# Pairing the lone tiles of batches 4 and 6, and another order in batch 0's token transform

## The chip, the cores and the metric

One core of one Trainium2 chip. The metric is the device time of one launch in microseconds; it is given as the median of several runs. PE is the matrix engine, ACT the scalar engine, DVE the vector engine, POOL the GpSimd engine, SP the engine that issues most DMAs. PSUM is the memory into which PE writes, eight banks of 512 fp32 columns.

## The reference, cut to what matters

Cosine attention over 8 batches, 12 heads, 448 tokens, 64 per head, then a Fourier mix over tokens and channels, then a layer norm and a two-layer perceptron with residual:

```python
q_n = q / (norm(q) + 1e-6);  k_n = k / (norm(k) + 1e-6)
attn = softmax(q_n @ k_n.T / tau);  x = attn @ v          # x: 8 x 448 x 768
u = x + real(fft(fft(x, axis=1), axis=2))                 # tokens, then channels
un = (u - mean(u)) / sqrt(var(u) + 1e-6)
out = u + relu(un @ w_ch1) @ w_ch2                        # 768 -> 3072 -> 768
```

## The kernel before, in words

All of it is one program that is unrolled in Python. Every step is an operation of a small planner (`Plan`): an engine or a choice of engines, a duration, a priority, the names it reads and writes. `Plan.schedule` runs a list scheduler over its own model of the engines and the DMA queues and writes out the order of the instructions of each engine by hand; `Plan.emit` then issues them in that order with semaphores between the engines. So each engine works its list strictly in order, and a late instruction holds up all behind it. The dictionary `SHIFT` adds a number to the priority of single operations, by name; `LATE` adds time to what the planner assumes of operations that wait for a DMA; `TIMES` holds the durations. `Plan.fill` puts dummy matmuls into gaps of PE.

For each batch b there are three parts.

*Attention, `attn(b)`.* Norms of q and k, loads by SP into STG (W2b and TX for batches 0 and 1), squares on ACT (L883), sums on DVE (L885), scaling on POOL into QH (L896), transposes by DMA. Then six head pairs, in the order `ORDER`: the scores are a matmul on 64 rows per head (L973), the exponentials are on ACT (L951), the products with v are L1004 and L1010, the division is on DVE, and `fold` (L1047, L1054, L1081) makes the sums and differences that the channel transform uses. The scores of a head pair come in steps: each step takes one large PSUM tile ("G", two banks, three of them) for each of its key tiles. Batches 1 to 3 take steps of two key tiles, which reach over to the next head pair, batches 4 to 7 steps of three.

*Fourier mix, `fft(b)`.* `fsum` (L1129 to L1138) is the token transform on PE, evacuated into Tt by ACT and DVE (L1160, the `te` operations); `fft` multiplies by the channel tables on PE (`fd0` and `fd1`, L1181 to L1191). In batch 0 each of `fd0` and `fd1` is two groups of matmuls, the cosine sums first and the sine sums second; both read the table CSd, whose negated sine part POOL writes (`sinp`, L659) from the plain sine table CSp. DVE adds the result to x and gives U with its row sums (L1233, in batch 0 L1245). Then each tile of 128 rows gets its mean (L1270), its sum of squares on ACT (L1275), logarithm and exponential for the root (L1278, L1280), and DVE centres and scales it into UN (L1282, `un`). In batch 0, tile 0, the scaling comes later and `un` only centres. UN lies in the buffer F and is transposed into UNT, by PE and two copies in batch 0 (L1292, L1300, `tn` and `eu`), by a DMA transpose on SP's queue in the others (L1303, `tru`). UNT has four slots of 128 columns.

*Perceptron, `ffn(b)`.* Tiles are worked in units of two tiles or one. Even batches have three tiles, odd ones four (their last tile, Zt, shares its buffer with the batch before). The up projection of a pair has 144 matmuls with 256 columns (`up`, L1350), that of a lone tile 144 with 128; the ReLU that evacuates them is on ACT or DVE (L1366). Three pairs at the end (the pair of batch 6 and both of batch 7) use `ups` (L1445), a Strassen scheme with 252 matmuls of 128 columns, whose weight sums DVE makes in `wsums` and `wsum3` in the buffers STG, QH and QK. The down projection (`prod`, L1494) takes seven products of 12 matmuls with 384 columns for a pair (Strassen again, with combinations of the hidden tiles on DVE, L1593, by `comb`), and four for a lone tile. Results of a pair are partly copied by ACT (L1514), added to by POOL (L1519) and by DVE (L1530) in `fin`, and stored by `store`: by SP, or by POOL as an indirect DMA (L1552).

`units` sets the slots, and `ffn` the units: a lone tile and a pair in batches 0 and 6, a pair and a lone tile in batches 2 and 4, two pairs in odd batches.

In `build` the program is laid out as attention of batch 0, then for each b the transform of b, the attention of b + 1 and the perceptron of b. The matmuls of the perceptron are one chain (`self.main`) with the lowest priority on PE, so they fill what attention and transform leave.

Of the kernel before, what the change touches and what calls it, by code (L numbers as in the profile page):

```python
# [7 lines left out]
AluOp = mybir.AluOpType  # L8
# [17 lines left out]
TF = 4  # L26
ORDER = (0, 1, 2, 3, 5, 4)
# [51 lines left out]

SHIFT = {  # L80
    "iotad": {0: 76.7149}, "tpd": {1: 15.2941}, "ktd0": {0: 169.0303}, "ix3": {0: -59.6164}, "ix4": {0: 735.3976}, "vz1": {0: 116.8365},
    "pads": {0: 761.6515}, "sins": {0: 15.0098}, "ldt0": {0: 217.8585}, "ldt1": {0: -95.8889}, "sind": {0: -207.551}, "sinp": {0: 240.8715},
# [418 lines left out]
class Kern:  # L501
# [663 lines left out]
    def fft(self, b):  # L1165
# [94 lines left out]
        for ui, ut in enumerate(order):  # L1260
# [24 lines left out]
            if b == 0 and ui == 0:  # L1285
                self.un0 = un
# [271 lines left out]
    def ffn(self, b):  # L1558
# [42 lines left out]
        for i, two in ((0, 0), (1, 1)) if b == self.nb - 2 else [(i, i + 1 < len(tiles)) for i in range(0, len(tiles), 2)]:  # L1601
            if two:
# [7 lines left out]
                for k in range(3):  # L1610
                    comb(4, 2, 3, [k], AluOp.add, "s1")
# [186 lines left out]
```

## Time and profile before

| | |
|---|---|
| runs | 577.16, 578.32, 577.0 us; median 577.16 |
| profiled execution | span 575.2 us from the first to the last instruction; the page gives no other time for it |
| PE busy | 555.8 us, of which 13.26 us are filler matmuls (L1737), nearly all before 48.3 us |
| DVE, ACT, POOL busy | 430.6, 385.3, 220.3 us |
| first up projection of batch 0 | 48.46 us |
| first matmul of batch 0's channel transform | 43.79 us |
| last down projection ends | 571.8 us |

A line of the page names the line of the program, the engine, the operation, what it writes and reads, shapes and count. In the rows of the order of an engine the first number is the start and the second the length. Matmuls are pipelined and their ends are modelled, so a single one's length in those rows is longer than the distance to the next; the rows of the chain that ended last give that distance over a run of them.

### The profile page before, as it was taken

How to read it: one execution, taken by the hardware profiler on the slowest of the kernel's cores; microseconds unless marked ns; L12 is line 12 of the kernel's file. 1: busy time of each engine (PE TensorE's matmuls, PEld its weight loads, DVE VectorE, ACT ScalarE, POOL GpSimd, SP SyncE). 2: the span in 40 equal slices, each digit the busy share in tenths (PEclk: the TensorE clock that was granted, in tenths of full speed). 3: DMA queues.
4: the chain of work that ended last, by engine and by line, in shares of the span. 5: the costliest groups of instructions: out<-in, count | busy, mean ns of one | idle time of the engine just before them, and what ended most of it. 6: DMA issues, size and time to landing. Idle time of an engine off the chain costs nothing.

```text
span 575.2 us, 16313 instructions
## 1 busy us (share of the span) xinstructions
PE 555.8 (97%) x6766; PEld 436.2 (76%) x6766; DVE 430.6 (75%) x917; ACT 385.3 (67%) x724; POOL 220.3 (38%) x332
## 2 busy tenths in 40 slices
PE   3899999999999999999999999999999999989997
PEld 3569787676787686878788787778778787959694
DVE  8989968996669869975669669776778579986262
ACT  7898885564876885687558875577637853747270
POOL 7534414356329544612370724523270210041303
PEclk9999999999999999999999999999999999999999
DMA  9999999975459739952595429743591210023001
GB/s 188 224 233 171 166 186 130 171 152 111 111 94 103 178 76 135 142 127 62 112 121 93 102 80 147 150 84 85 89 113 29 43 57 28 2 43 72 28 28 56
DMA packets 187898, 62.20 MB, mean 108 GB/s; under 512 B 166800, under 2 KB 185616, under 8 KB 187824
## 3 DMA queue, kind: packets, MB, share of 16 engines
q1 hardware_dynamic: 129856, 38.35, 33.7%
q0 software_dynamic: 57968, 22.81, 30.9%
q8 instruction: 53, 0.87, 0.6%
q14 instruction: 21, 0.17, 0.1%
HBM read 51.90 MB, written 11.01 MB: 109 GB/s over the span
## 4 chain that ended last, share of the span: by engine, by line
PE 60%; DVE 4%; ACT 2%; issue 0%; DVEq 0%; ACTq 0%
PE PS L1494 23%; PE PS L1350 20%; PE PS L1445 6%; PE PS L1010 4%; PE PS L973 3%; DVE U L1233 1%; PE PS L1004 1%; PE PS L986 1%; ACT E L951 1%; DVE ACG L1222 1%; ACT F L1275 1%; PE PS L1134 1%; PE PS L1191 1%; DVE SM L885 1%; DVE HQ L1593 1%
## 5 line engine op out<-in xcount | busy, mean ns | idle before, releaser
L1350 PE MATMUL PS<-UNT,W1b 128*128 128x256 bf16 (+1 forms) x1872 | 186.1, 256 | 1.2 <-DMA UNT<-F 0.6
L1350 PEld LDWEIGHTS PS<-UNT,W1b 128*128 128x128 bf16 x1872 | 155.5, 98 | 20.1 <-issue 2.7
L951 ACT ACTIVATE E<-PS 128x900 bf16<-128x900 f32 (+1 forms) x192 | 148.0, 827 | 19.1 <-PE PS L973 16.6
L1494 PE MATMUL PS<-W2b,HQ 128*128 128x384 bf16 x768 | 133.1, 326 | 0.0
L896 POOL TENSOR_TENSOR QH<-STG,SM 128x256 bf16<-128x256 f32 x126 | 82.3, 679 | 91.9 <-DVE SM L702 73.3
L1494 PEld LDWEIGHTS PS<-W2b,HQ 128*128 128x128 bf16 x768 | 73.3, 98 | 46.2 <-issue 0.7
L1519 POOL TENSOR_TENSOR OUTB<-OUTB,U 128x192 f32<-128x192 f32 x66 | 43.2, 675 | 138.5 <-ACT OUTB L1514 137.3
L1366 ACT ACTIVATE HQ<-PS 128x512 bf16<-128x512 f32 x81 | 48.2, 595 | 40.0 <-PE PS L1350 39.5
L1494 PE MATMUL PS<-TX,HQ 128*128 128x384 bf16 (+2 forms) x408 | 69.7, 321 | 1.8 <-ACT MV L1278 1.6
L883 ACT ACTIVATE QH<-STG 128x384 f32<-128x384 f32 x84 | 42.7, 520 | 25.8 <-DVE SM L885 21.3
L1494 PEld LDWEIGHTS PS<-TX,HQ 128*128 128x128 bf16 x408 | 38.4, 98 | 25.7 <-ACT MV L1278 2.0
L1593 DVE TENSOR_TENSOR HQ<-HQ 128x1536 bf16<-128x1536 bf16 (+1 forms) x69 | 49.5, 721 | 9.9 <-ACT HQ L1366 7.1
L885 DVE TENSOR_REDUCE SM<-QH 128x6 f32<-128x384 f32 x84 | 44.7, 544 | 11.3 <-ACT QH L883 11.0
L1010 PE MATMUL PS<-VB,E 128*128 128x65 bf16 x1152 | 51.4, 193 | 0.0
L1366 DVE TENSOR_SCALAR HQ<-PS 128x512 bf16<-128x512 f32 x45 | 31.0, 688 | 23.8 <-PE PS L1350 23.4
L1010 PEld LDWEIGHTS PS<-VB,E 128*128 128x128 bf16 x1152 | 47.7, 97 | 1.2
L1552 POOL DMA_INDIRECT out_dram<-OUTB,IDX x21 | 23.8, 1134 | 56.9 <-DVE OUTB L1530 51.7
L1004 PE MATMUL PS<-VZ,E 128*128 128x130 bf16 x192 | 41.6, 219 | 0.5 <-ACT E L951 0.2
L973 PE MATMUL PS<-QK 64*128 64x225 bf16 (+2 forms) x864 | 39.6, 227 | 0.1
L1233 DVE SCALAR_TENSOR_TENSOR U<-ACG,X 128x768 bf16<-128x768 f32 (+4 forms) x39 | 39.1, 1015 | 0.8
L1530 DVE TENSOR_TENSOR OUTB<-PS,OUTB 128x384 f32<-128x384 f32 x33 | 18.2, 553 | 25.7 <-PE PS L1494 21.9
L1514 ACT ACTIVATE OUTB<-PS 128x384 f32<-128x384 f32 x33 | 16.1, 488 | 29.5 <-PE PS L1494 29.1
(191 smaller groups left out, 793.6 us busy)
## 6 DMA issues: line engine op xcount, KB each, us to landing
STG<-in_q_dram SPq DMA_DIRECT2D x18, 384.0 KB, 4.0
STG<-in_k_dram SPq DMA_DIRECT2D x18, 384.0 KB, 3.8
VB<-in_v_dram POOLq DMA_DIRECT2D x24, 192.0 KB, 7.1
W1b<-in_moe_w_ch_dram POOLq DMA_DIRECT2D x12, 384.0 KB, 7.7
W2b<-in_moe_w_ch_dram POOLq DMA_DIRECT2D x12, 384.0 KB, 7.2
out_dram<-OUTB SPq DMA_DIRECT2D x7, 384.0 KB, 3.4
W2b<-in_q_dram SPq DMA_DIRECT2D x2, 576.0 KB, 10.0
W2b<-in_k_dram SPq DMA_DIRECT2D x2, 576.0 KB, 10.7
```

What stands on the lines that cost most here:

```text
L885: P.add("dve", lambda v, o=SS[:, i, H // ns * x:H // ns * (x + 1)], sq=sq: v.tensor_reduce(o, sq.rearrange("p (h d) -> p h d", d=DH), AX.X ...
L896: r = v.tensor_tensor(v3(qh)[:, h:h + 4], v3(buf)[:, h:h + 4], RN[:, i, h:h + 4].unsqueeze(2).to_broadcast((128, 4, DH)), AluOp.mult)
L951: return a.activation(o, self.PS[:, bk:bk + nc_, 0:SQ2], ACTF.Exp, scale=1.0 / self.tau)
L973: i = pe.matmul(self.PS[:, bk + h, c0:c0 + n], self.KT[r, jj, kt * 128:(kt + 1) * 128], self.QT[r, jj, cols], start=True, stop=True)
L1004: r = pe.matmul(o, st(6), self.VZ[:, j, :], start=not split, stop=(split and i == 0), skip_group_check=True)
L1010: r = pe.matmul(o[:, 65 * h:65 * h + 65], st(2 * kt + h), self.VB[:, kt, 2 * j + h, :], start=(split and i == h == kt == 0), stop=((not sp ...
L1233: self.snu.append(P.add("dve", lambda v: v.scalar_tensor_tensor(two(U[o0:o0 + n, ut, :]), src, 1.0, two(X[i0:i0 + n, x, :]), AluOp.mult, A ...
L1350: r = pe.matmul(self.PS[:, bk, x * n:(x + 1) * n], self.W1b[:, j, ft * 128:(ft + 1) * 128], self.UNT[:, j, cs], start=(j == 0), stop=(j == ...
L1366: return e.activation(o, i, ACTF.Relu) if e is self.nc.scalar else e.tensor_relu(o, i)
L1494: r = pe.matmul(self.PS[:, bk, 0:n], lhs(f), rhs(f), start=(start and f == 0), stop=(stop and f == NF // 2 - 1), skip_group_check=True)
L1519: r = g.tensor_tensor(self.OUTB[:, ob, xs], self.OUTB[:, ob, xs], self.U[:, ut, xs], AluOp.add)
L1593: P.add("dve", lambda v: v.tensor_tensor(cs(o), cs(a), cs(bq), op), 0.16 + 0.3 * len(ks), -0.5, f"{nm}{ks[0]}_{b}", reads=rd, writes=[x fo ...
```

## The change

1. *Units.* `units` now goes through all tiles in order and makes pairs, except for the tiles in `ONES`, batch 0's first and batch 2's first, which stay alone. A pair may reach from a batch into the next. Batch 2 has its lone tile ahead of its pair. Batch 4's third tile is paired with batch 5's first, batch 5's second with its third, batch 5's fourth with batch 6's first. A unit belongs to the batch of its last tile. `fin` and `store` take the batch of the tile.
2. *The held tile.* Batch 5's fourth tile (`HELD`) isn't centred in `fft(5)`; `unheld` does it after the up projection of the pair ahead, into one of the six QH buffers in place of UN, with its transpose on SP's queue.
3. *Batch 0's transform.* The sine sums, which read CSp, come first in `fd0` and `fd1`; the negated table gets a name of its own, CSm, for which only the other groups wait.
4. *Halves.* Batch 0's first tile is centred in two halves of 384 columns, transposed in two groups of three matmuls, and each copy waits for its own group.
5. *Scores of batch 3* come in steps of three key tiles.
6. *Order.* `LATE` assumes later DMAs for four kinds of operations; the first scores of a batch are ordered behind the last channel transform matmuls of the batch before; `QUEUES` pins the order of the first loads on SP's and POOL's queues; `SHIFT` has entries for nearly all operations of all batches, so that the lists of all engines are drawn anew. One write of the tail's output (`finz`) names one buffer more.

```diff
+ONES = ((0, 0), (2, 0))
+HELD = (5, 3)
...
+QUEUES = [("ld_q1_0 ld_k0_0 ld_q0_0 ld_t0_0 ld_q2_0 ld_t1_0 ld_k1_0 ld_t2_0 ld_k2_0 ld_q0_1 ld_t0_1 ld_k0_1 ld_k1_1 ld_t1_1 ld_q1_1"),
+          ("ld_v2_0 ld_v0_0 ld_v1_0 ld_v3_0 W1_0 W1_1 W1_2 W1_3 W1_4 W1_5 W1_6 W1_7 W1_8 W1_9 W1_10")]
...
-LATE = {r"W[12]_\d+": 1.5, "tmd": 2.0, r"sq\d_\d": 1.5, ... r"ktd\d": 2.0, r"qdup\d": 2.0, ...
+LATE = {r"sq6_[2-7]": 4.0, r"W[12]_\d+": 1.5, "tmd": 2.0, r"sq\d_\d": 2.0, ... r"ktd\d": 3.5, r"qdup\d": 4.0, ...
...
-            ... "sinp", reads=["CSp"], writes=["CSd"])
+            ... "sinp", reads=["CSp"], writes=["CSm"])
...
-            elif b >= 4:
+            elif b >= 3:
                 steps = [[(pos, kt) for kt in range(3)]]
...
-                      ... order=([self.last_qk] if self.last_qk else []) + self.pvs[-2:-1])
+                      ... order=([self.last_qk] if self.last_qk else []) + self.pvs[-2:-1] + (self.fd_ops[-1:] if b and pos == 0 else []))
...
-            for sg in (0, 1) if b == 0 else (0,):
+            for sg in (1, 0) if b == 0 else (0,):
                 self.fd_ops.append(P.add("pe", ..., f"fd{kt}_{b}",
-                                         reads=["Tt0", "Tt1", "Tt1b", "CSd"] + (["CSp"] if b == 0 and sg else []),
-                                         tiles=(tile,), acquire=None if sg else tile, margin=0.2))
+                                         reads=["Tt0", "Tt1", "Tt1b", "CSd"] + ([["CSm"], ["CSp"]][sg] if b == 0 else []),
+                                         tiles=(tile,), acquire=tile if sg or b else None, margin=0.2))
...
-            fds = self.fd_ops[-2:]
+            fds = self.fd_ops[-2:][::-1]
...
+            if (b, ui) == HELD:
+                self.held = (ut, rn, lp, slot, col)
+                continue
+            halves = [slice(0, 384), slice(384, DM)] if late else [slice(0, DM)]
+            for g, c in enumerate(halves):
+                un = P.add("dve", lambda v, ...: v.tensor_scalar(self.UN[:, nb_, c], U[:, ut, c], self.MV[:, ut, 0:1], ...), ... f"un{ui}_{b}", ...)
             if b == 0:
                 tile = Tile("G")
+                tns = []
+                for g in range(2) if late else (None,):
+                    def fn(pe, tile=tile, nb_=nb_, g=g):
+                        for j in range(NJ) if g is None else range(3 * g, 3 * g + 3):
+                            r = pe.matmul(...)
+                    tns.append(P.add("pe", fn, 0.2 if late else 0.4, lp, f"tn{ui}_{b}", ...))
                 for g in range(2):
...
-                    self.evac(ev, 384, lp, f"eu{ui}{g}_{b}", writes=[f"uT{slot}" + "xy"[g]], after=(tile.users[0],), tiles=(tile,))
+                    self.evac(ev, 384, lp, f"eu{ui}{g}_{b}", writes=[f"uT{slot}" + "xy"[g]], after=(tns[g if late else 0],), tiles=(tile,))
...
+    def unheld(self):
+        P = self.P
+        ut, rn, lp, slot, col = self.held
+        b, ui = HELD
+        r = self.qh_next % 6
+        self.qh_next += 1
+        qn = [f"QH{r}"] + ["QH1x"] * (r == 1) + ["QH4x"] * (r in (3, 4))
+        P.add("dve", lambda v: v.tensor_scalar(self.QH[:, r, :], self.U[:, ut, 0:DM], self.MV[:, ut, 0:1], self.RS[:, ut:ut + 1], AluOp.add, AluOp.mult),
+              t_dve(DM, 4) + 0.16, lp, f"un{ui}_{b}", reads=rn + [f"MV{ut}", f"RS{ut}"], writes=qn)
+        self.last_tru = P.add("sp", lambda sy, sem: sy.dma_start_transpose(self.UNT[:, :, col:col + 128], self.QH[:, r, :]).then_inc(sem, 16), ...)
...
-        self.slots, u = [], 0
-        for b in range(self.nb):
-            sl = []
-            for n in (1, 2) if b in (0, self.nb - 2) else (2, 2) if b % 2 else (2, 1):
-                sl += [2 * (u % 2) + x for x in range(n)]
-                u += 1
-            self.slots.append(sl)
+        self.slots = [[0] * len(self.tiles(b)) for b in range(self.nb)]
+        order = [(b, i) for b in range(self.nb) for i in range(len(self.tiles(b)))]
+        u = x = 0
+        self.pairs = []
+        while x < len(order):
+            n = 1 if order[x] in ONES else 2
+            for y in range(n):
+                b, i = order[x + y]
+                self.slots[b][i] = 2 * (u % 2) + y
+            self.pairs.append(order[x:x + n])
+            u, x = u + 1, x + n
...
-        for i, two in ((0, 0), (1, 1)) if b == self.nb - 2 else [(i, i + 1 < len(tiles)) for i in range(0, len(tiles), 2)]:
+        for k, unit in enumerate([u for u in self.pairs if u[-1][0] == b]):
+            two = len(unit) == 2
...
-                if b >= self.nb - 2:
+                if b == self.nb - 1 or unit[0] == (self.nb - 2, 1):
                     if not last_b:
                         self.wsum3()
...
-                    self.up(b, (i, i + 1), chunks, True)
+                    self.up(b, unit, chunks, True)
+                    if unit[1][0] == HELD[0] and unit[0][0] < b:
+                        self.unheld()
...
+        named = {op.name: op for op in self.P.ops if op.dma is not None}
+        for q in QUEUES:
+            q = [named[n] for n in q.split()]
+            for x, y in zip(q, q[1:]):
+                y.order += (x,)
```

More of the change, by code (lines that the diff above doesn't have):

```diff
@@ L977, in attn @@
                 self.last_qk = P.add("pe", fn, 0.195 * len(st_) + 0.2, pj, f"qk{j}{st_[0][1]}_{b}", reads=rd,
-                      tiles=new, acquire=new, margin=0.3, order=([self.last_qk] if self.last_qk else []) + self.pvs[-2:-1])
+                      tiles=new, acquire=new, margin=0.3, order=([self.last_qk] if self.last_qk else []) + self.pvs[-2:-1] + (self.fd_ops[-1:] if b and pos == 0 else []))
                 for tile, (ps, kt) in zip(new, st_):
@@ L1055, in fold @@
                        t_dve(512, 2) + (0.03 if b else 0.0), pj, f"f{eo}{dj}_{b}", reads=["AC0", "AC2"],
-                       writes=[f"F{eo}{dj}"] + ([f"UN{x}" for x in range(4)] if dj == 0 and eo == 0 else []),
+                       writes=[f"F{eo}{dj}"] + ([f"UN{x}{y}" for x in range(4) for y in ("", "h")] if dj == 0 and eo == 0 else []),
                        after=[self.first_f] if dj or eo else [])
@@ L1285, in fft @@
-            if b == 0 and ui == 0:
-                self.un0 = un
+            if (b, ui) == HELD:
[3 more added lines that the diff above has]
+            for g, c in enumerate(halves):
+                un = P.add("dve", lambda v, ut=ut, nb_=nb_, late=late, c=c: v.tensor_scalar(self.UN[:, nb_, c], U[:, ut, c], self.MV[:, ut, 0:1], None if late else self.RS[:, ut:ut + 1],
+                                                                                          AluOp.add, AluOp.bypass if late else AluOp.mult),
+                      t_dve(c.stop - c.start, 4) + 0.16, lp, f"un{ui}_{b}", reads=rn + [f"MV{ut}"] + [f"RS{ut}"] * (not late), writes=[f"UN{nb_}" + "h" * g] + [f"UN{nb_}h"] * (not late))
@@ L1287, in fft @@
             if b == 0:
                 tile = Tile("G")
-                def fn(pe, tile=tile, nb_=nb_):
-                    for j in range(NJ):
-                        r = pe.matmul(self.PS[:, self.bank(tile) + j // 3, 128 * (j % 3):128 * (j % 3) + 128],
-                                      self.UN[:, nb_, 128 * j:128 * j + 128], self.ID, start=True, stop=True)
-                    return r
-                P.add("pe", fn, 0.4, lp, f"tn{ui}_{b}", reads=[f"UN{nb_}", "ID"], tiles=(tile,), acquire=tile)
+                tns = []
@@ new lines, in fft @@
+                for g in range(2) if late else (None,):
+                    def fn(pe, tile=tile, nb_=nb_, g=g):
+                        for j in range(NJ) if g is None else range(3 * g, 3 * g + 3):
+                            r = pe.matmul(self.PS[:, self.bank(tile) + j // 3, 128 * (j % 3):128 * (j % 3) + 128],
+                                          self.UN[:, nb_, 128 * j:128 * j + 128], self.ID, start=True, stop=True)
+                        return r
+                    tns.append(P.add("pe", fn, 0.2 if late else 0.4, lp, f"tn{ui}_{b}", reads=[f"UN{nb_}" + "h" * (g == 1), "ID"] + [f"UN{nb_}h"] * (g is None), tiles=(tile,), acquire=None if g else tile))
@@ L1337, in up @@
         P = self.P
-        sl = [self.slots[b][i] for i in idx]
+        sl = [self.slots[x][i] for x, i in idx]
         n = 128 * len(sl)
@@ L1531, in fin @@
         on = f"OUT{ob}" + "b" * c + "z" * (c0 > 0)
-        return self.P.add("dve", fn, t_dve(c1 - c0), -1, f"{nm}_{b}", reads=([on] if src == "out" else self.unames(b, ut)) + [f"RS{ut}"] * late, writes=[on],
+        return self.P.add("dve", fn, t_dve(c1 - c0), -1, f"{nm}_{b}", reads=([on] if src == "out" else self.unames(bt, ut)) + [f"RS{ut}"] * late, writes=[on],
                           after=(op,), tiles=(tile,))
@@ L1562, in ffn @@
         if b == 0:
-            self.up(0, (0,), range(0, NF, 4), False)
-            self.up(0, (1, 2), range(0, NF, 2), True)
+            self.up(0, ((0, 0),), range(0, NF, 4), False)
+            self.up(0, ((0, 1), (0, 2)), range(0, NF, 2), True)
             for i, ut in enumerate(tiles):
@@ L1614, in ffn @@
                 op = self.prod(b, b1, H(0), W(0, 0), hr(0), wr(0), f"m1{i}", True, False)
-                rd = self.fin(b, b1, op, 0, 0, u0, "a", f"fa{i}")
+                rd = self.fin(b, b1, op, 0, 0, u0, "a", f"fa{i}", bt=b0)
                 comb(0, 4, 0, range(3), AluOp.subtract, "s2")
                 op = self.prod(b, ta, H(1), W(1, 0), hr(1), wr(1), f"m2{i}", True, True)
-                self.fin(b, ta, op, 0, 0, u0, "out", f"fin{i}0")
-                if last_b and i + 2 == len(tiles):
-                    self.store(b, i, u0, 0, 0)
+                self.fin(b, ta, op, 0, 0, u0, "out", f"fin{i}0", bt=b0)
+                if lone:
+                    self.store(b0, i, u0, 0, 0)
                 comb(1, 1, 0, range(3), AluOp.subtract, "s4")
                 op = self.prod(b, b1, H(0), TT(1), hr(0), tr(2), f"m6{i}", False, False, rd)
-                rd = self.fin(b, b1, op, 0, 1, u0, "a", f"fv{i}")
+                rd = self.fin(b, b1, op, 0, 1, u0, "a", f"fv{i}", bt=b0)
                 op = self.prod(b, tb, H(4), TT(0), hr(4), tr(1), f"m5{i}", True, False)
@@ L1628, in ffn @@
                 rd = self.fin(b, b1, op, 1, 1, u1, "out", f"fin{i + 1}1")
-                if last_b and i + 2 == len(tiles):
+                if lone:
                     self.store(b, i + 1, u1, 1, 1)
                 op = self.prod(b, tb, H(1), W(1, 1), hr(1), wr(1), f"m3{i}", False, True, rd2)
-                self.fin(b, tb, op, 0, 1, u0, "out", f"fin{i}1")
-                self.store(b, i, u0, 0, 1 if last_b and i + 2 == len(tiles) else None)
-                if last_b and i + 2 == len(tiles):
+                self.fin(b, tb, op, 0, 1, u0, "out", f"fin{i}1", bt=b0)
+                self.store(b0, i, u0, 0, 1 if lone else None)
+                if lone:
                     tz, cz = Tile("G"), slice(256, 384)
                     pre = P.add("dve", lambda v: v.tensor_tensor(self.OUTB[:, 1, cz], self.PS[:, self.bank(b1), cz], self.U[:, u1, cz], AluOp.add), t_dve(128), -1,
-                                f"finz_{b}", reads=self.unames(b, u1), writes=["OUT1z"], after=(m7,), tiles=(b1,))
+                                f"finz_{b}", reads=self.unames(b, u1), writes=["OUT1z", "OUT1"], after=(m7,), tiles=(b1,))
                     op = self.prod(b, b1, H(3), lambda f: self.TX[:, 2, f, 0:256], hr(3), tr(4), f"m4{i}", False, True, rd, n=256, more=[pre])
@@ L1649, in ffn @@
                 continue
-            u0 = tiles[i]
-            self.up(b, (i,), (0, 12, 4, 16, 8, 20), False)
+            self.up(b, unit, (0, 12, 4, 16, 8, 20), False)
             comb(4, 0, 2, range(3), AluOp.add, "s5")
```

40 lines of the change are left out of this document (22 added, 18 removed), and 503 rows, old and new, of tables (SHIFT, TIMES).

## The prediction

> **What bounds the kernel now.** I read the profile's page first: the busy shares and the clock in 40 slices.
>
> ```profile
> span 575.2 us, 16313 instructions
> PE 555.8 (97%) x6766; PEld 436.2 (76%) x6766; DVE 430.6 (75%) x917; ACT 385.3 (67%) x724; POOL 220.3 (38%) x332
> PEclk9999999999999999999999999999999999999999
> ```
>
> PE is busy for 97% of the span, and the granted clock stays at full speed, so idle time or work on PE is what can be taken away. That busy time counts filler matmuls too, so next I asked for the windows by stage, PE's own waits from 48 us on, and the order of PE, ACT, DVE and POOL around the first up projection.
>
> ```profile
> 48.40:117.90 69.50, 68.15 (x790) 52.67 (x789) 57.80 (x136) 51.87 (x107) 26.04 (x37) 1.00 1.12 161
> 117.90:194.90 77.00, 76.73 (x787) 58.01 (x788) 60.40 (x118) 52.47 (x100) 40.66 (x51) 1.00 0.73 120
> 333.20:368.40 35.20, 35.20 (x374) 27.56 (x372) 25.57 (x55) 19.47 (x35) 17.24 (x25) 1.00 0.84 101
> 368.40:388.30 19.90, 19.82 (x302) 15.76 (x300) 15.58 (x39) 15.21 (x35) 4.15 (x7) 1.00 0.53 127
> 484.60:516.10 31.50, 29.86 (x371) 24.15 (x369) 28.29 (x64) 20.62 (x48) 5.53 (x7) 1.00 0.16 27
> 571.80:575.20 3.40, 0.00 (x0) 0.00 (x0) 0.29 (x1) 0.00 (x0) 0.27 (x1) 0.88 0.32 116
> ...
> PE PS L1494 <- ACT MV L1278: 1.6, 1, 1.6
> PE PS L1350 <- DMA UNT<-F: 0.6, 1, 0.6
> ```
>
> In a window row the first pair is length and PE busy, then PE loads, DVE, ACT, POOL. Idle PE time between 48.4 and 571.8 adds up to 1.35 + 0.27 + 0.08 + 1.64 and some tenths, 3.5 us in all, and the two longest waits are 2.2 us of it. So the time is: the 48.4 us until the first up projection, some 520 us of matmuls with hardly a hole, and a 3.4 us tail. A matmul that goes away saves its length, as long as the chains on DVE and ACT keep feeding PE.
>
> **The change, part by part.** The sum is made against the span of 575.2 us; the median of the three runs, 577.16, is 1.96 above it, and I carry these 1.96 over. Prices of matmuls come from the chain that ended last, where they stand back to back:
>
> ```profile
> 236.98 4.03 PE PS L1350 x72
> 301.38 9.17 PE PS L1350 x84
> 530.30 13.65 PE PS L1494 x84
> 203.68 0.49 PE PS L973 x8
> 322.65 0.71 PE PS L973 x24
> 204.17 1.42 PE PS L1350 x12
> 213.01 1.31 PE PS L1350 x12
> ```
>
> *Down projection.* A lone tile takes 4 products of 12 matmuls, a pair 7. Batch 4's third tile now goes with batch 5's first, batch 5's fourth with batch 6's first, and the pair (batch 5's tiles 1 and 2) stays a pair: two lone tiles and two pairs become three pairs. 2 x 48 + 2 x 84 = 264 matmuls become 252. At 13.65/84 = 162.5 ns that is -1.95 us.
>
> *Up projection.* The two lone tiles took 288 matmuls with 128 columns, 4.03/72 = 56.0 ns each, 16.1 us; the pair that replaces them takes 144 with 256, 9.17/84 = 109.2 ns each, 15.7 us: -0.4 us. The Strassen form of the up projection stays with the same three pairs.
>
> *Scores of batch 3.* Nine groups of 8 matmuls become six of 12, as batches 4 to 7 have them. 9 x 0.49 - 6 x 0.71 = 0.15 us, and three fewer returns to the up projection, which takes 1.42 instead of 1.31 us for 12 matmuls just behind a group, 3 x 0.11: -0.5 us together. Such a group takes all three large PSUM tiles at once, which batches 4 to 7 do with PE full.
>
> *Start of batch 0's transform.* Both table halves used to wait for the negated table of POOL (L659); now the half that needs only the plain table goes first.
>
> ```profile
> 41.17 2.17 POOL L659 TENSOR_SCALAR CS<-TX 128x770 bf16<-128x770 bf16 x1 [0.31 <-ACT TX L647]
> 42.03 1.33 ACT L1159 ACTIVATE E<-PS 128x900 bf16<-128x900 f32 x2
> 43.79 0.84 PE L1181 MATMUL PS<-CS,E 128*128 128x193 bf16 x8
> 46.56 0.42 DVE L1282 TENSOR_SCALAR F<-U,MV 128x768 bf16<-128x768 bf16 x1
> 48.46 7.79 PE L1350 MATMUL PS<-UNT,W1b 128*128 128x128 bf16 x126
> ```
>
> POOL ends at 43.34, but ACT's evacuation, which the transform needs anyway, ends at 43.36: the first matmul can come from 43.79 to about 43.4, no further. Centring in halves lets three transposes and the first copy begin after the first half. A half takes between 0.21 and 0.42 us, half the row and all of it, so this gains from 0.2 us to nothing. The up projection starts up to 0.6 us earlier. How much of it arrives? The wait of 0.6 us for the transposes of batch 1's tiles (UNT<-F, near 117 us) says that batch 1's chain is already the later one there, with DVE busy 57.8 of 69.5 us. Bounds 0 and -0.6; I take -0.3, the middle, since the rows stand as near to the one as to the other.
>
> *Holes.* The planner's priorities, and so nearly every engine's order, are drawn anew. The 3.5 us of holes can go or stay; nothing in this trace shows which. The largest, 1.64 us, sits where batch 6's last pair meets batch 7's transform and DVE has 28.3 us of work in 31.5. Batch 6 then has a whole pair ahead of that pair in place of a lone tile, so its weight sums can be made earlier. I take half of this hole, -0.8; bounds 0 and -3.5.
>
> *What lies beside.* Per pair in place of two lone tiles DVE gets 4 more combinations, POOL 6 halves of additions, ACT 3 copies:
>
> ```profile
> L1593 DVE TENSOR_TENSOR HQ<-HQ 128x1536 bf16<-128x1536 bf16 (+1 forms) x69 | 49.5, 721 | 9.9 <-ACT HQ L1366 7.1
> L1519 POOL TENSOR_TENSOR OUTB<-OUTB,U 128x192 f32<-128x192 f32 x66 | 43.2, 675 | 138.5 <-ACT OUTB L1514 137.3
> ```
>
> That is 2.9 us on DVE and 4.1 on POOL, costed at nothing, like the three copies, because by the window rows DVE idles between 333 and 388 us for 14 of 55 us, ACT for 20 and POOL for 34. Without that cover DVE's 2.9 us would be the price. Batch 5's held tile is centred into another buffer and transposed later, so on SP's queue its transpose moves past loads of a later batch, and behind it wait loads only; the tile is needed a whole pair (about 40 us) later, the transpose's landing is 2.8 us, so again nothing. Lone before pair in batch 2 asks for one tile instead of two when that batch starts; PE has only 0.27 us of hole up to there, so it gains at most that. The pinned queue orders and the extra ordering behind the last transform repeat an order that the trace already shows on SP, so nothing.
>
> Sum: -1.95 - 0.4 - 0.5 - 0.3 - 0.8 = -3.95, span 571.25, time 573.2.
>
> **The rivals.** *Batch 5 comes late (slower).* Until now the lone tile of batch 4 covered PE while batch 5's transform was finished:
>
> ```profile
> 365.26 1.06 DVE L1233 SCALAR_TENSOR_TENSOR U<-ACG,X 128x768 bf16<-128x768 f32 x1
> DMA to landing us min/median/max: 2.7/2.8/5.3
> 368.42 4.44 PE L1350 MATMUL PS<-UNT,W1b 128*128 128x128 bf16 x72
> 388.30 2.79 PE L1350 MATMUL PS<-UNT,W1b 128*128 128x256 bf16 x24
> 371.38 0.94 ACT L1275 ACTIVATE F<-U,MV 128x768 bf16<-128x768 bf16 x1 [0.24 <-DVE MV L1270]
> 380.32 0.28 ACT L1278 ACTIVATE MV<-MV 128x1 f32<-128x1 f32 x1
> 380.64 0.20 ACT L1280 ACTIVATE MV<-MV 128x1 f32<-128x1 f32 x1
> 380.88 0.48 DVE L1282 TENSOR_SCALAR F<-U,MV 128x768 bf16<-128x768 bf16 x1 [0.22 <-ACT MV L1280]
> ```
>
> After the change the pair with batch 5's first tile is due when batch 4's pair ends, at 368.4 less the 0.8 us saved ahead of it, 367.6. With the transform where it is, the shortest way for that tile is addition, squares, logarithm, root, centring and transpose, 365.26 + 1.06 + 0.94 + 0.28 + 0.20 + 0.48 + 2.8 = 371.0, so 3.4 us of idle PE, less what batch 6's scores fill. Against it: PE ends batch 5's scores at 342.3 but begins its first sums only at 356.95, so there is room to pull the transform forward.
>
> ```profile
> 341.61 0.71 PE PS L973 x24
> 356.95 0.41 PE PS L1134 x8
> ```
>
> What would make it worse is POOL: the same DVE addition took 1.35 us at 366.25 while POOL multiplied, 0.96 at 435.99 while POOL stood idle.
>
> ```profile
> 366.25 1.35 DVE L1233 SCALAR_TENSOR_TENSOR U<-ACG,X 128x768 bf16<-128x768 f32 x1
> 364.33 2.47 POOL L896 TENSOR_TENSOR QH<-STG,SM 128x256 bf16<-128x256 f32 x3
> 435.99 0.96 DVE L1233 SCALAR_TENSOR_TENSOR U<-ACG,X 128x768 bf16<-128x768 f32 x1
> ```
>
> With six more POOL pieces, at 0.4 us each, up to 2.4 us of DVE time would be lost there, and the wait is 5.8 us. Against the safe terms of 3.15 us that gives 577.16 - 3.15 + 5.8 = 579.8; without the slowdown 577.4, no change. It is slower from 4.9 us of wait on. The Trainium skill, page "GPSIMD Engine Reference", section "1. Specifications", has GpSimd's memory interfaces shared with VectorE, contended with two-input DVE instructions; these rows fit it, and it speaks against adding POOL work.
>
> *The saving is lost elsewhere (same).* PE's work falls by 2.85 us, but chains on DVE and ACT do not get shorter; new waits of 1.5 to 2.5 us at the batch boundaries give 576.5. For it: DVE and ACT already hold 6% of the chain that ended last.
>
> ```profile
> PE 60%; DVE 4%; ACT 2%; issue 0%; DVEq 0%; ACTq 0%
> ```
>
> Against it: where PE runs through the pairs of batch 4 the window row has no hole at all.
>
> *All holes go.* 577.16 - 2.85 - 0.6 - 3.5 = 570.2. For it: every order is new; against it: the same DVE load.
>
> *Narrow matmuls wait for their weights.* A load takes 98 ns by itself:
>
> ```profile
> L1350 PEld LDWEIGHTS PS<-UNT,W1b 128*128 128x128 bf16 x1872 | 155.5, 98 | 20.1 <-issue 2.7
> ```
>
> Were the lone tiles' matmuls paced by it, they would cost 288 x 98 ns = 28.2 us, the up term would be -12.5 and the time 577.16 - 1.95 - 12.5 - 0.5 - 1.1 = 561.1. Against it: 72 of them took 4.03 us, so the loads run beside the matmuls. The Trainium skill, page "TensorE: Matmul & The Clock Gate", section "Back-to-back issue gap", takes a middle way, about 81 ns for 128 columns in a stream of loads and matmuls: by it the up term would be -7.6 and the time about 566. This trace disagrees with it, with 56.0 ns.
>
> **How the numbers follow.** Forecast 573.2 (between 571.5 and 575.2): 0.64. All holes go: 0.14. Lost elsewhere: 0.12. Batch 5 late: 0.09. Narrow matmuls paced by loads: 0.01. About 0.3%, 1.7 us, is what a measurement of this kernel tells from no change. Faster is the forecast, the third and the last rival, 0.79; same 0.12; slower 0.09. The range takes in the case without holes down to 570.2, and most of the same-case, to 576.8; that leaves out the late batch, the narrow matmuls and parts of the edges.
>
> **What would show it.** The trace after has 12 matmuls fewer on the line of the down projection and 144 fewer on that of the up projection, and batch 3's scores come in six groups; the first up projection starts before 48.2; between 360 and 375 us PE has no hole of over 1 us; its holes from 48 us to the tail are under 3 us. I would be wrong if PE waited for a transpose of batch 5's first tile, for ACT or DVE at a batch's start, or if the first up projection came no earlier.

## The result and the profile after

The changed kernel took 574.71 us in the median (574.34, 575.18, 573.9, 575.07), the kernel before, beside it, 577.74: ratio 0.9934, 95% interval 0.9922 to 0.9947. It is 3.0 us faster; 573.2 was forecast, a gain of 3.95. The profiled execution took 574.34 us with a span of 572.5. The head of its page:

```profile
span 572.5 us, 15993 instructions
PE 552.2 (96%) x6598; PEld 432.6 (76%) x6598; DVE 439.6 (77%) x926; ACT 382.8 (67%) x723; POOL 231.5 (40%) x338
```

The sum is checked with one window, from the first matmul of the first up projection to the end of PE's last. The kernel before, then the one after (first pair: length, PE busy):

```profile
48.46:571.70 523.24, 519.81 (x6249) 408.39 (x6248) 387.03 (x814) 343.77 (x658) 192.60 (x275) 1.00 0.60 99
```

```profile
48.46:570.06 521.60, 517.29 (x6092) 405.57 (x6092) 396.15 (x824) 341.42 (x658) 204.60 (x281) 1.00 0.68 99
```

Length less busy is the sum of PE's holes, span less the window's end is the tail:

| us | before | after | difference | forecast |
|---|---|---|---|---|
| until the first up projection | 48.46 | 48.46 | 0.0 | -0.3 |
| PE busy | 519.81 | 517.29 | -2.5 | -2.85 |
| holes of PE | 3.43 | 4.31 | +0.9 | -0.8 |
| behind PE's last matmul | 3.47 | 2.47 | -1.0 | 0 |
| span | 575.2 | 572.5 | -2.7 | -3.95 |

Of the 2.7 us by which the profiled span is shorter, 1.6 lie between the first up projection and PE's last matmul (523.24 to 521.60), where the sum had 3.65, and 1.0 lie behind it.

The work of PE is there nearly as counted. The next rows are groups by line and shape of the kernel after: the up projection has 1440 + 288 matmuls where there were 1296 + 576, the down projection 1212 in 720 + 420 + 48 + 12 + 12 (two small last forms, not shown) where there were 1224.

```profile
L1758 PE MATMUL PS<-UNT,W1b 128*128 128x256 bf16 x1440 | 167.9, 273 | 0.7 <-ACT KTD L1230 0.4 <-DVE MV L1657 0.3
L1902 PE MATMUL PS<-W2b,HQ 128*128 128x384 bf16 x720 | 124.8, 326 | 0.0
L1902 PE MATMUL PS<-TX,HQ 128*128 128x384 bf16 x420 | 74.6, 326 | 1.6 <-DVE OUTB L1939 1.4 <-DVE HQ L2002 0.3
L1758 PE MATMUL PS<-UNT,W1b 128*128 128x128 bf16 x288 | 17.4, 219 | 0.5 <-DMA UNT<-F 0.3 <-ACT UNT L1691 0.2
L1902 PE MATMUL PS<-W2b,TX 128*128 128x384 bf16 x48 | 8.1, 326 | 0.0
```

PE's own waits inside that window, after the change (total, times, longest):

```profile
PE PS L1902 <- DVE OUTB L1939: 1.4, 2, 1.0
PE PS L1521 <- DVE F L1485: 0.7, 1, 0.7
PE PS L1758 <- ACT KTD L1230: 0.4, 1, 0.4
PE PS L1758 <- DVE MV L1657: 0.3, 1, 0.3
PE PS L1758 <- DMA UNT<-F: 0.3, 1, 0.3
```

The 1.64 us ahead of batch 7 is gone altogether. In its place stand smaller waits at places that had none. Two of them show what feeds them. Timeline rows of the kernel after around the longest, DVE, POOL and PE (start, length; idle time before and its releaser in brackets):

```profile
189.82 0.56 DVE L1939 TENSOR_TENSOR OUTB<-PS,OUTB 128x384 f32<-128x384 f32 x1 [1.70 <-POOL OUTB L1928]
...
182.83 3.75 POOL L1283 TENSOR_TENSOR QH<-STG,SM 128x256 bf16<-128x256 f32 x4
186.72 2.99 POOL L1928 TENSOR_TENSOR OUTB<-OUTB,U 128x192 f32<-128x192 f32 x4
...
190.44 1.31 PE L1902 MATMUL PS<-TX,HQ 128*128 128x384 bf16 x7 [1.01 <-DVE OUTB L1939]
```

PE waits for DVE's output addition, that one for POOL's, and POOL's stood behind four scalings of the next batch. These additions are of batch 1, whose two pairs are the same before and after; only their place in POOL's order is new. The second is PE's 0.7 us for L1485. The eight executions of that line that read F, by duration (min, median, max):

```profile
L1485 DVE TENSOR_TENSOR F<-F x8: 348/354/770, 291.6 to 485.2; 128x388 bf16<-128x388 bf16 x8
```

The slowest ended just ahead of that wait, at 356 us, while POOL multiplied from 352.9 to 357.4; in the kernel before the same eight took 355 to 368 ns. That agrees with the Trainium skill, page "GPSIMD Engine Reference", section "1. Specifications", by which GpSimd's memory interfaces are shared with VectorE, and VectorE instructions with two inputs are among those that contend for them; no run here moved the POOL work away to prove it.

### The profile page after: what moved, and what is told of

It is laid out like the page before. It is cut to its first block, busy times and chain, and to the rows that moved or that the text cites. A ratio compares the mean times of both kernels' runs of the same rounds, so it can differ in the third digit from the quotient of the medians.

```text
span 572.5 us, 15993 instructions
## 1 busy us (share of the span) xinstructions
PE 552.2 (96%) x6598; PEld 432.6 (76%) x6598; DVE 439.6 (77%) x926; ACT 382.8 (67%) x723; POOL 231.5 (40%) x338
## 4 chain that ended last, share of the span: by engine, by line
PE 75%; DVE 17%; ACT 5%; issue 2%; POOL 1%; DMA 0%; DVEq 0%; POOLq 0%; ACTq 0%
PE PS L1902 26%; PE PS L1758 26%; PE PS L1853 6%; PE PS L1397 6%; PE PS L1360 5%; DVE U L1620 3%; DVE HQ L2002 2%; PE PS L1391 2%; ACT E L1338 2%; PE PS L1373 1%; DVE ACG L1609 1%; PE PS L1525 1%; DVE U L1632 1%; DVE OUTB L1939 1%; DVE SM L1272 1%
## 5 line engine op out<-in xcount | busy, mean ns | idle before, releaser
L1902 PE MATMUL PS<-W2b,HQ 128*128 128x384 bf16 x720 | 124.8, 326 | 0.0
L1283 POOL TENSOR_TENSOR QH<-STG,SM 128x256 bf16<-128x256 f32 x126 | 87.4, 720 | 90.9 <-DVE SM L1089 64.7
L1928 POOL TENSOR_TENSOR OUTB<-OUTB,U 128x192 f32<-128x192 f32 x72 | 50.8, 725 | 127.0 <-ACT OUTB L1923 125.8
L1902 PEld LDWEIGHTS PS<-W2b,HQ 128*128 128x128 bf16 x720 | 68.8, 98 | 43.3 <-issue 0.6
L1902 PE MATMUL PS<-TX,HQ 128*128 128x384 bf16 (+2 forms) x444 | 76.7, 322 | 1.6 <-DVE OUTB L1939 1.4
L1902 PEld LDWEIGHTS PS<-TX,HQ 128*128 128x128 bf16 x444 | 41.4, 98 | 28.2 <-DVE OUTB L1939 2.5
L2002 DVE TENSOR_TENSOR HQ<-HQ 128x1536 bf16<-128x1536 bf16 (+1 forms) x73 | 55.1, 758 | 9.1 <-ACT HQ L1774 6.3
L1662 ACT ACTIVATE F<-U,MV 128x768 bf16<-128x768 bf16 x28 | 26.2, 934 | 21.2 <-DVE MV L1657 17.8
L1923 ACT ACTIVATE OUTB<-PS 128x384 f32<-128x384 f32 x36 | 17.6, 488 | 29.5 <-PE PS L1902 29.2
```

Source lines behind the costliest of these rows:

```text
L1283: r = v.tensor_tensor(v3(qh)[:, h:h + 4], v3(buf)[:, h:h + 4], RN[:, i, h:h + 4].unsqueeze(2).to_broadcast((128, 4, DH)), AluOp.mult)
L1902: r = pe.matmul(self.PS[:, bk, 0:n], lhs(f), rhs(f), start=(start and f == 0), stop=(stop and f == NF // 2 - 1), skip_group_check=True)
L1928: r = g.tensor_tensor(self.OUTB[:, ob, xs], self.OUTB[:, ob, xs], self.U[:, ut, xs], AluOp.add)
L2002: P.add("dve", lambda v: v.tensor_tensor(cs(o), cs(a), cs(bq), op), 0.16 + 0.3 * len(ks), -0.5, f"{nm}{ks[0]}_{b}", reads=rd, writes=[x fo ...
```

## The experiments

**The same kernel again, and work taken out or put in with all orders kept.** The planner writes the orders from its own durations, so an edit at the emission of the matmuls leaves every order as it was.

> The changed kernel once more, unaltered, for a second profile. If the shorter stretch behind PE's last matmul (2.43 us against 3.49 in the kernel before) is part of the change, it is 2.4 again, the holes of PE sum to 4.3 us again, the first up projection starts at 48.5 us again, and the ratio is 0.993. If any of the three is a matter of the single execution, it moves by some tenths here, and the tail is somewhere between 2.4 and 3.5 us.

Measured: 575.4 against 578.82 us, ratio 0.9945 (0.9931 to 0.9958). Span 572.5, tail 2.49, holes 4.5 us, of which 1.00 and 0.66 at the same two places; the first up projection at 48.01 instead of 48.46. So tail and holes belong to the program, and the start moves by itself.

```diff
                 for f in range(4 * c, 4 * c + 4):
+                    if nm[0] == "y" and b in (4, 6) and f == 4 * c + 1:
+                        continue
```

> The kernel before with 24 matmuls of 384 columns left out of the down projections of the two lone tiles of batches 4 and 6 (one of each group of four; those tiles' output is incomplete), all orders as they were. Theory 'PE's work passes through': 24 x 162.5 ns = 3.9 us less, ratio 0.9932. Rival 'the chains on DVE and ACT set these stages': new waits of PE take back at least half, 0 to 2 us less, ratio 0.9965 to 1.

Measured: 577.5 us, ratio 0.9986 (0.9969 to 1.0003): 0.8 us, not 3.9 (1.3 by the medians, 577.5 and 578.82). From the first up projection to PE's last matmul its profile is 0.7 us shorter, and PE's holes there are 5.5 us instead of 3.4. The timeline of PE in this run shows where the rest went:

```profile
369.93 4.45 PE L1350 MATMUL PS<-UNT,W1b 128*128 128x128 bf16 x72
...
383.21 0.78 PE L973 MATMUL PS<-QK 64*128 64x128 bf16 x24 [0.38 <-ACT E L951]
385.51 0.22 PE L1004 MATMUL PS<-VZ,E 128*128 128x130 bf16 x1 [0.44 <-issue]
388.92 2.79 PE L1350 MATMUL PS<-UNT,W1b 128*128 128x256 bf16 x24
...
483.51 2.17 PE L1445 MATMUL PS<-UNT,W1b 128*128 128x128 bf16 x36
486.35 1.26 PE L1445 MATMUL PS<-KTD,QH 128*128 128x128 bf16 x18 [0.66 <-ACT E L1454]
506.83 4.06 PE L1496 MATMUL PS<-TX,HQ 128*128 128x384 bf16 x24 [1.64 <-ACT MV L1278]
516.58 3.62 PE L1445 MATMUL PS<-UNT,W1b 128*128 128x128 bf16 x62
```

Batch 4's lone tile takes 18.99 us instead of 19.88 (368.42 to 388.30 before): 0.9 of 1.95 arrive; most of the rest are a wait for ACT's exponentials and one at 385 us that the profile doesn't name. Batch 6's lone tile is done in the full 1.95 us less, but from there to batch 7's first pair it is 33.07 us instead of 31.47 (484.60 to 516.07): 1.6 of the 1.95 are given back. The one new wait that the profile names there is 0.66 us for ACT's evacuation of the Strassen sums (E, L1454); the 1.64 us for ACT's MV is as long as before. So in the old order a matmul saved at a lone tile was worth little: 'PE's work passes through' fails there.

> The changed kernel with 24 matmuls of 384 columns added (12 ahead of the fifth product of each of the two joined pairs, overwritten by that product), all orders as they were. Theory 'PE's work passes through': 3.9 us more than the changed kernel, ratio to the kernel before 1.000. Rival 'PE waits for DVE and ACT in these stages': the extra work fills holes there (0.3 + 0.0 us stand on the profile between 411 and 484 us, 0.3 in the stretch ahead), and under 2 us arrive, ratio 0.9965 or less.

```diff
+                if (nm, b) in (("m50", 5), ("m50", 6)) and c == 0:
+                    for f in range(12):
+                        pe.matmul(self.PS[:, bk, 0:n], lhs(f % 4), rhs(f % 4), start=True, stop=False, ...)
```

Measured: 579.47 us, ratio 1.001 (1.000 to 1.002), 4.1 us above the unaltered copy in the same comparison. All 3.9 us arrive: no hole in the joined pairs takes up added work. That is one half of the comparison only. Matmuls left out of the joined pairs, and matmuls added to the lone tiles of the kernel before, were not run, so it isn't shown that a saved matmul is worth more in the new order than in the old.

**One part at a time, orders drawn anew.** A run for each of: joining alone with the old priorities; all edits with the old priorities, margins and free queues; the change without the joining (`ONES` with (4, 2) and (6, 0) added, `HELD` off); the change with batch 2's lone tile behind (`ONES = ((0, 0), (2, 2))`). The first still names the table's negated half CSm and keeps one ordering edge of the change, that of a batch's first scores.

> The kernel before with the two lone tiles joined to the tiles of the next batch and nothing else: its own priorities, batch 2's lone tile behind its pair, nine groups of scores in batch 3, the old start. PE has 2.35 us less to do (1.95 down, 0.4 up). Theory 'the work passes through by itself': holes of PE stay at 3 to 4 us, span 572.8, ratio 0.996. Rival 'it needs the orders redrawn': the old priorities on the joined units leave new waits of PE of 2.4 us or more in the stretch from batch 4's last pair to batch 7, ratio 1.000 or more. The stretch behind PE's last matmul stays 3.5 us if the ordering of the last store pieces is what shortened it.

> The changed kernel with all its edits but the priorities, lateness margins and unpinned queues of the kernel before. PE's work is that of the changed kernel, 2.7 us less than before. Theory 'the work passes through by itself': holes 3.5 to 5 us, ratio 0.993 to 0.996. Rival 'it needs the orders redrawn': holes of 7 us or more, ratio 1.000 or more. The tail is 2.5 us if it is the ordering of the last store pieces, 3.5 if it is the drawn order.

> The changed kernel with the joining alone undone: batches 4 and 6 have their lone tiles again, all else (priorities by name, batch 2, scores, start) as changed. PE's work rises by 2.35 us. Theory 'the work passes through': ratio to the kernel before 0.9945 + 2.35/577 = 0.9986. Theory with the chain behind the lone tile of batch 6 (24 matmuls left out gained 1.3 of 3.9 us because PE then waited there for ScalarE and VectorE): the 1.6 us wait ahead of batch 6's last products comes back too, ratio 1.001 to 1.003. Rival 'the gain lies in the new orders and not in the joining': ratio 0.995 as the changed kernel.

> The changed kernel with batch 2's lone tile behind its pair again. The work of PE is the same to 0.1 us. Where the changed kernel waits 1.01 us (189.4 us, for an output addition of batch 1) and 0.30 (193.3, for the transposed tile of batch 2), the holes change: if putting the lone tile first is what opened the 1.01 us hole, it goes and the ratio is 0.993; if it saved a wait for two tiles, a hole of 0.5 to 2 us opens at batch 2's start and the ratio is 0.996 to 0.998; if both are the orders' own, holes differ by under 1 us with no pattern there.

| | median us | ratio, interval | fillers after the first up projection |
|---|---|---|---|
| joining alone | 612.49 | 1.0590 (1.0565 to 1.0616) | 420 |
| old orders | 668.36 | 1.1551 (1.1532 to 1.1569) | 1314 |
| joining undone | 584.63 | 1.0105 (1.0089 to 1.0122) | 90 |
| lone behind | 656.45 | 1.1335 (1.1316 to 1.1353) | 1218 |

All four are slower than the kernel before, by 6 to 90 us. The rival 'it needs the orders redrawn' was on the right side, but none of the expectations came near the size. The busy time of PE misleads here. The window from first up projection to last matmul of the joining alone, and its group of fillers:

```profile
49.44:607.10 557.66, 545.57 (x6507) 429.53 (x6506) 391.82 (x821) 343.89 (x658) 201.76 (x281) 1.00 0.57 93
```

```profile
L1773 PE MATMUL PS<-W1b 128*128 128x128 bf16 x420 | 27.2, 220 | 1.3 <-DVE ACG L1226 0.8 <-DVE U L1237 0.3
```

PE looks busy for 26 us more than before with less to do: the program puts filler matmuls where the planner foresees a hole, 420 here, 6 in both kernels of the case. Idle PE is holes and fillers together, the time in which PE runs a filler or nothing: 3.8 us before, 4.6 after, 37 with the joining alone, 93 with the old orders, 84 with the lone tile behind, 11.6 with the joining undone. In the joining alone they lie at 350 to 400 us (162), 450 to 475 (156) and 525 to 550 (96), the transitions into batches 5, 6 and 7. With the joining undone 84 of the 90 lie between 500 and 525 us, behind batch 6's lone tile, where the kernel before had its 1.64 us. So these four runs don't price the joining or the other edits: the priorities are fitted to one graph, and on a neighbouring graph they lose far more than is at stake. What makes them no clean trial is the names. `SHIFT` goes by an operation's name and its place among those of the same name, and names hold batch and unit, so where the units change, entries fall on other operations or on none. With the joining undone 45 of the 2663 entries of the changed kernel find no operation, most of them of the unit that held batch 6's first tile; with the lone tile behind it is 42, all of batch 2's perceptron; in the first two runs it is 4 and 10 of the 338 old ones (counted in the kernels). How much of the loss comes from that isn't known. A run with the units as before and priorities fitted to them anew wasn't made. What new orders are worth without the joining, and the joining with orders fitted to it but nothing else, stays open.

**The start.** After the schedule is drawn, the waits of the old start are added again:

```diff
         self.est = self.P.schedule()
+        nth("fd0_0", 0).deps.add(nth("sinp", 0))
+        nth("tn0_0", 0).deps.add(nth("un0_0", 1))
+        nth("eu00_0", 0).deps.add(nth("tn0_0", 1))
```

> The changed kernel, orders as they are, with the waits put back that its new start had taken away: the first group of batch 0's transform waits for the negated table as well, the first three transposes wait for both halves of the centring, and both copies for all six transposes. By the profile the table (done 43.74 us) is there as soon as ScalarE's evacuation (43.76), so that wait costs nothing; the transposes come 0.2 us later and ScalarE's copy, at 47.94 behind a sum of squares, not at all: theory 'the start's edits are covered' gives 0 to +0.1 us on the start of the first up projection. Rival 'they are worth the 0.3 us of the prediction and something else ate it': +0.3 us.

Measured: 575.41 us, ratio 0.9941 (0.9928 to 0.9954), the same as the copy without them. Rows of the changed kernel, ACT's evacuation ahead of the transform, POOL's table, PE's first transform matmul, the transposes, the up projection:

```profile
43.23 0.53 ACT L1546 ACTIVATE E<-PS 65x450 bf16<-65x450 f32 x1
...
41.57 2.17 POOL L1046 TENSOR_SCALAR CS<-TX 128x770 bf16<-128x770 bf16 x1 [0.90 <-ACT TX L1034]
...
43.81 0.34 PE L1568 MATMUL PS<-TX,E 128*128 128x193 bf16 x2
47.01 0.56 PE L1683 MATMUL PS<-TX,F 128*128 128x128 bf16 x6 [0.30 <-DVE F L1674]
48.46 1.24 PE L1758 MATMUL PS<-UNT,W1b 128*128 128x128 bf16 x19 [0.22 <-ACT UNT L1691]
```

The first transform matmul now stands 0.05 us behind the evacuation, where it stood 0.43 behind; with the wait for the table put back it is 0.14, so that wait is worth 0.09 us. The rest is filler. PE's fillers ahead of the transform, in the kernel before and in the changed one:

```profile
41.91 0.50 PE L1737 MATMUL PS<-TX 128*128 128x128 bf16 x6
42.58 1.37 PE L1737 MATMUL PS<-TX 128*128 128x128 bf16 x18 [0.17 <-DVE SM L762]
43.79 0.84 PE L1181 MATMUL PS<-CS,E 128*128 128x193 bf16 x8
```

```profile
42.74 1.18 PE L2156 MATMUL PS<-TX 128*128 128x128 bf16 x18 [0.28 <-DVE SM L1149]
```

Before, the table was there at 43.34, and PE ran fillers without a hole until the transform began at 43.79: 24 of them against 18 after. Six fillers at the 56 ns of a matmul with 128 columns are 0.34 us. They stood there because the planner's own times put the table behind the evacuation, and it fills the holes that it foresees.

From the first transform matmul to the up projection it is 4.65 us, as before (4.67), so the halves gave nothing beside the old centring. From the evacuation's end to the up projection it is 4.70 to 4.85 us in the eight profiles with the changed start, 4.96 with the waits put back and 5.10 to 5.19 in the five with the old start: some 0.4 us are gained. But the evacuation itself ended anywhere from 42.7 to 44.7 us over the 14 profiles, in copies of one kernel too (43.76 and 43.31), so these 0.4 us are lost in the spread.

**The tail.** In both kernels POOL's last indirect store follows an addition of DVE. DVE's addition and the store, before and after:

```profile
569.76 0.56 DVE L1530 TENSOR_TENSOR OUTB<-PS,OUTB 128x384 f32<-128x384 f32 x1 [1.19 <-PE PS L1494]
...
571.09 0.97 POOL L1552 DMA_INDIRECT out_dram<-OUTB,IDX  x1 [3.55 <-DVE OUTB L1530]
```

```profile
568.12 0.56 DVE L1939 TENSOR_TENSOR OUTB<-PS,OUTB 128x384 f32<-128x384 f32 x1 [1.20 <-PE PS L1902]
...
568.95 0.98 POOL L1961 DMA_INDIRECT out_dram<-OUTB,IDX  x1 [3.02 <-DVE OUTB L1939]
```

0.77 us from the addition's end to the store before, 0.27 after. By their operands in the trace, the store has three semaphores to wait for: one is in the store itself, two are in a wait instruction ahead of it. Before, DVE's is in the one ahead, after, in the store. (The Trainium skill, page "Perfetto Trace Analysis", section "Identifying Dependency Chains", says that such instructions may be put ahead; it gives no price.) The program names the waits in the order of an unordered set, so this is nobody's choice: two other runs that have the changed kernel's tail have it once inside (lone tile behind, tail 2.46 us) and once ahead (joining undone, 3.01). The edits sort them, for the last store or, in the last two runs, for all instructions (latest named last):

```diff
-                    for key, val in need.items():
+                    for key, val in sorted(need.items(), key=lambda x: (when.get(x[0], 0.0), x[0])):
```

> The kernel before with one thing changed: POOL's last indirect store names its three waits in another order, so that the late one, for VectorE's addition, is carried by the store itself instead of by the wait instruction ahead of it. Theory 'the tail of the changed kernel is the place of that wait': the store starts 0.27 us after the addition instead of 0.77, POOL's drain ends about 1.0 us sooner, the stretch behind PE's last matmul is 2.5 us instead of 3.47, ratio 0.9983. Rival 'the tail belongs to another part of the change': 3.47 us, ratio 1.000.

> The changed kernel with the opposite edit: the wait for VectorE is moved to the wait instruction ahead of POOL's last store. Theory 'place of the wait': tail 3.0 to 3.5 us instead of 2.47, ratio to the kernel before 0.9955 to 0.9963. Rival: 2.47 us, ratio 0.9945 as before.

> The changed kernel with every instruction's waits named in the order in which the planner expects them to be fulfilled, so that on every engine the instruction itself carries the latest one; nothing else is changed. Theory 'only POOL's last store hangs on it': tail 2.47 us as it is, holes of PE 4.3 to 5.2 us as in the three profiles with these orders, ratio 0.9945. Rival 'a wait in an instruction of its own costs some tenths on every engine, and part of the new holes are that': holes 3.5 us or less, ratio 0.993 or less.

> The kernel before with the same ordering of waits on every instruction. Theory 'only POOL's last store hangs on it': tail 2.5 us, holes 3.4 us with the one of 1.64 us ahead of batch 7 still there, ratio 0.9983; then the joining and the redrawn orders are worth 0.9945 / 0.9983 = 0.9962, 2.2 us, on equal terms. Rival: the holes shrink as well, ratio 0.997 or less.

I had the direction wrong: the instruction carries the wait that is named first. So the two edits of the one store left each kernel's store as it was (tails 3.56 and 2.47 us, ratios 1.0011, 1.0002 to 1.0020, and 0.9944, 0.9931 to 0.9958) and tested nothing. But naming the latest last everywhere moved the changed kernel's wait out of the store:

```profile
569.80 0.56 DVE L1941 TENSOR_TENSOR OUTB<-PS,OUTB 128x384 f32<-128x384 f32 x1 [1.12 <-PE PS L1904]
...
571.17 0.98 POOL L1963 DMA_INDIRECT out_dram<-OUTB,IDX  x1 [3.52 <-DVE OUTB L1941]
```

0.81 us, and the tail is 3.12 us. Over all 14 profiles, the six with the wait for DVE inside the store have a tail of 2.46 to 2.49, the eight with it ahead 3.0 to 3.6. That the place of the wait costs 0.5 us at the store and 0.55 to 0.65 in the tail is shown. The further 0.45 us between the changed kernel so altered (3.12) and the kernel before in its four profiles (3.45 to 3.60) lie in POOL's last instruction, its drain. It ends 0.59 to 0.63 us after the store has landed in the eight profiles with the changed kernel's priorities, and 1.08 to 1.12 in the six with the old ones, one of which (old orders) has all other edits. So they go with the priorities; by what way isn't known. The times: changed 576.43 us, ratio 0.9962 (0.9935 to 0.9988), before 579.14, ratio 1.0019 (1.0010 to 1.0028). With waits sorted alike in both, and their stores alike too, the change is 0.9962 / 1.0019 = 0.9943, by the two intervals some 0.3% to either side: the change stays faster with them alike, though a share of 0.6 us couldn't be told. PE's holes were 4.5 and 4.1 us, against 4.3 and 3.4 with the waits as they fell, so these two runs don't put the new holes down to the place of waits either. The opposite sorting, earliest named last, which by this should help both kernels, wasn't run.

## Why the prediction was right, and where its terms were off

The direction was right, and 574.71 us lies in the band of the forecast, 571.5 to 575.2. That it does is luck in part: between the first up projection and PE's last matmul the sum had -3.65 us and 1.64 came, and 1.0 us came from the tail, for which the sum had nothing. Without it the time would be 575.7, outside that band, though inside the wider range down to 570.2 and up to 576.8 that the prediction names as well.

*Work of PE: right in size, not shown why it arrived.* 2.5 of 2.85 us came, and 0.9 of them went into holes. I argued that it arrives because PE has hardly a hole. That step failed where it was tried: with 24 matmuls less in the same lone tiles of the kernel before at most 1.8 of 3.9 us arrived (by the interval). A stage without holes can still have its DVE and ACT chains right behind. That it arrives after the change because lone tiles became pairs and the orders were drawn for them is argued, not shown: 24 matmuls added there cost their full 3.9 us, but none were left out.

*Holes: the mis-sized term.* -0.8 forecast, +0.9 measured. The named hole went fully (1.64, not half). The cover that was named for it fits, since fillers stand there with the joining undone, but that run also lost priorities in that unit. And 2.5 us of new holes came at other places. The longest comes from POOL's output additions, and not from the six new ones that I had costed at nothing: it stands in batch 1, where no work was added, so it belongs to the new order. The statement "holes under 3 us" failed, with 4.3; "none over 1 us between 360 and 375" held, with 0.3 for `MV`. Of the signs of being wrong, two came in this profile: PE waited for DVE ahead of batch 5's transform (0.7 us), and the first up projection came no earlier.

*Start.* The bound of 0.4 us from the evacuation was met (0.43 to 0.05), but not as I read it: the table was there 0.45 us ahead of the transform, and PE was running fillers. The halves' 0 to 0.2 were 0. The up projection came no earlier in that profile, because everything ahead of it was 0.4 us later; "before 48.2" failed by that chance (48.01 in the second profile).

*Tail.* -1.0 us that the sum had no term for: 0.55 to 0.65 for the place of one wait, which nobody chose, and some 0.45 that go with the priorities. It covers part of the 1.7 us that the holes were off.

*The rivals.* "Batch 5 late" came with the 0.3 us for `MV` only; what comes nearest to it is the joining with the old priorities, with fillers at 350 to 400 us. "Lost elsewhere" came in part, 2.5 us of new waits as it priced, beside a hole that went. The narrow matmuls were not paced by loads: PE's work fell by 2.5 us and not by 15. That orders drawn from priorities of another graph could cost tens of microseconds was in none of them.

## What to carry to other kernels

A saved matmul is worth its length only where the chains on the other engines leave room: take some out with the order kept, as a trial, before restructuring for it. In a program whose orders come from fitted priorities a run that keeps the fit of another graph doesn't price an edit, so judge edit and fit together, fit both sides, and count fillers as idle time. A gap ahead of a matmul can be full of fillers: look there before it is put down to a wait. Look at the last store: which of its waits it carries itself was worth half a microsecond here.

## What the runs showed that was not expected

A wait in an instruction ahead of POOL's store released it 0.77 to 0.81 us after the event, one in the store itself 0.27. The first up projection began between 47.6 and 49.7 us over 14 profiles, with 0.45 us between two of one kernel, and what followed took up the difference (PE's end 570.06 and 570.00). In the slowest run, with 1314 fillers, the granted clock stood at 1.0 and PE at 95% busy, while for 93 us between the first up projection and its last matmul it ran fillers or nothing.
